# Moving one token tile from the dense group to the last Strassen group of a linear-attention and expert-mixture kernel

## The chip, the cores and the metric

The kernel runs on one core of one Trainium2 chip. The metric is the device time of one execution in microseconds, as the median of three runs.

## The reference

Linear attention over 4 batches, 8 heads, 576 positions and head size 64, followed by a dense mixture of 4 experts over the 2304 resulting tokens. Cut to what matters:

```python
def phi(x):
    proj = einsum('bhsd,df->bhsf', x, w_phi)              # 128 features
    proj = proj - max(abs(proj), axis=-1, keepdims=True)
    return concatenate([exp(proj), exp(-proj)], axis=-1)

q_p, k_p = phi(q), phi(k)
kv, z = einsum('bhsf,bhsd->bhfd', k_p, v), sum(k_p, axis=2)
x = einsum('bhsf,bhfd->bhsd', q_p, kv) / (einsum('bhsf,bhf->bhs', q_p, z)[..., None] + 1e-6)

x = x.transpose(0, 2, 1, 3).reshape(2304, 512)            # tokens x model width
p = domain_probs / (domain_probs.sum(-1, keepdims=True) + 1e-9)
for e in range(4):                                        # w1: 512 x 1024, w2: 1024 x 512
    out += p[:, e:e+1] * (maximum(x @ w1[e], 0) @ w2[e])
```

## The kernel before, in words

The 2304 tokens are 18 tiles of 128. The mixture walks over the hidden width in units: a unit is 256 hidden columns of one expert, so a pass over all experts has NU = 16 units. The tokens are split into three groups, and each group makes one pass of 16 units: units 0 to 15 for the first group, 16 to 31 for the second, 32 to 47 for the last.

- The first group (`first_units`, L586) has N0 = 4 tiles, computed densely. A unit has 2 halves of 128 hidden columns, for each half 4 slices of the model width, for each slice 3 matmuls (`terms`, L94: every factor is split into a high and a low part, and three of the four products are kept). That is 24 first-layer matmuls over 512 token columns (`l1_part`, L574). Each half ends with a relu on ScalarE (L598) and the low part of it on VectorE (`relu_lo`, L567).
- The second group (`xa`) has 8 tiles, the last (`xb`) 6. Their first layer is a Strassen-Winograd product over two halves of the tokens, 512 or 384 columns each (`strassen_unit`, L679): 7 products, named A to D by their PSUM bank, each of 2 x 3 matmuls, 42 in all. VectorE, GpSimd and ScalarE make sums of the products, the relus and the low parts (`evacuate`).
- The second layer is the same everywhere (`l2_tile`, L532): 6 matmuls of 512 columns for each tile of 128 tokens, then one VectorE operation that scales the bank by the token's probability and adds it to the output (L555). The second layer of unit n is issued during unit n + 1, from a list `pend`. In a Strassen unit one tile is issued behind each product from the second on, and what is left follows the seventh.

The first group shares TensorE with the attention. Attention is a list of steps for 16 pairs of heads (`STAGES`, L406), each with a due key; a pair has 16 keys, and pairs 0 to 3, the first batch, have to be through before the first group begins. The queue of due steps is worked off as a clock advances (`tick`, L450). The clock's step is set (L878) so that the attention from pair 4 on is spread over 88% of the ticks of the first group; a dense unit has 8 ticks for its first layer and 2 for each second-layer tile. Weight loads and their splits into parts are also placed by ticks (`load`, `convert`, W_WAIT, L67): the load of w2 for unit n + 1 goes 4 ticks behind the first layer of unit n, its split begins at the end of unit n. What each engine executes, and SyncE's DMA queue too, is in the order in which this clock issues it.

The operands of the Strassen groups (differences of token halves, T1 to T4) are made by `x_ops` (L627) on VectorE, ScalarE and GpSimd from `xd`, a copy of the attention's output in DRAM. For the second group they are issued near the end of the attention and in its first unit; for the last group in the last two units of the second. From unit 16 on `s_sums` (L474), `s_hi` and `s_lo` make the sums of weight blocks for the Strassen products, on the same three engines.

The PSUM banks: `ps_l1` 2, `ps_l2` 2, `ps_att` 3, `ps_kv` 1. Products A and B and the dense first layer use `ps_l1`; C and D use `ps_att`. Second-layer tiles use `ps_l2`; in the dense units after the attention they go by their index to `ps_l2`, `ps_att`, `ps_kv`, `ps_att`; in the Strassen units every tile whose number is a multiple of 3 goes to `ps_kv`.

The activations h of a unit lie in tiles of 128 x 2 x 512: one for each token half and for high and low part, two buffers of each.

Of the kernel before, what the change touches and what calls it, by code (L numbers as in the profile page):

```python
# [11 lines left out]
F32 = mybir.dt.float32  # L12
F32R = mybir.dt.float32r
# [7 lines left out]
def kernel(  # L21
# [25 lines left out]
    NTT = NT // P  # L47
    NPAIR = B * NP

    N0, N1 = 4, 4  # L50

# [18 lines left out]
    const = ctx.enter_context(tc.tile_pool(name="const", bufs=1))  # L70
    dram = ctx.enter_context(tc.tile_pool(name="dram", bufs=1, space=bass.MemoryType.DRAM))
    wp = ctx.enter_context(tc.tile_pool(name="wp", bufs=1))
    hp_ = ctx.enter_context(tc.tile_pool(name="hp", bufs=2))
    ps_l1 = ctx.enter_context(tc.tile_pool(name="ps_l1", bufs=2, space=PSUM))
    ps_l2 = ctx.enter_context(tc.tile_pool(name="ps_l2", bufs=2, space=PSUM))
    ps_att = ctx.enter_context(tc.tile_pool(name="ps_att", bufs=3, space=PSUM))
# [4 lines left out]
    pr = const.tile([P, NTT, NE], F32, name="pr")  # L81
    prs = const.tile([P, NTT], F32, name="prs")
    const.tile([P, 24], F32, name="gap")
    x0_hi = const.tile([P, NP, N0 * P], F32R, name="x0_hi")
    x0_lo = const.tile([P, NP, N0 * P], F32R, name="x0_lo")
    x1_hi = const.tile([P, NP, N1 * P], F32R, name="x1_hi")
    x1_lo = const.tile([P, NP, N1 * P], F32R, name="x1_lo")
    out0 = const.tile([P, N0, DM], F32, name="out0")
    xd = dram.tile([NP, P, NT], F32, name="xd")
    den_d = dram.tile([NPAIR, 2, S], F32, name="den_d")  # L90
    rec_d = dram.tile([NPAIR, 2, S], F32, name="rec_d")
# [440 lines left out]
    def l2_tile(n, h, j, tile, o):  # L532

        e = (n % NU) * 2 // NFC
        if n >= NU and tile % 3 == 0:
            ps = ps_kv.tile([P, DM], F32, name="l2", tag="kv")
        elif n < NU and clock.key > LAST_PS:

            pool, tag = ((ps_l2, "l2"), (ps_att, "att"), (ps_kv, "kv"), (ps_att, "att"))[j]
            ps = pool.tile([P, DM], F32, name="l2", tag=tag)  # L540
        else:
            ps = ps_l2.tile([P, DM], F32, name="l2", tag="l2")
        for f in range(2):
            for k, (l, r) in enumerate(terms(h, weights["w2", n])):
                nc.tensor.matmul(  # L545
                    ps, lhsT=l[:, f, j * P : (j + 1) * P], rhs=r[:, f, :],
                    start=(f == 0 and k == 0), stop=(f == 1 and k == 2),
                )
            if f == 0 and n < NU:
                tick()  # L550
        p = pr[:, tile, e : e + 1]
        if n % NU == 0:
            nc.vector.tensor_scalar_mul(o, ps, p)
        else:
            nc.vector.scalar_tensor_tensor(o, ps, p, o, op0=ALU.mult, op1=ALU.add)  # L555
        if n % NU == NU - 1:
            nc.sync.dma_start(out[tile * P : (tile + 1) * P, :], o)
# [16 lines left out]
    def l1_part(n, f, k):  # L574

        if k == 0:
            banks[n, f] = ps_l1.tile([P, 512], F32, name="l1", tag="l1")
        ksl = slice(k * P, (k + 1) * P)
        w1 = [t[:, f] for t in weights["w1", n]]
        for j, (l, r) in enumerate(terms(w1, (x0_hi, x0_lo))):  # L580
            nc.tensor.matmul(
                banks[n, f], lhsT=l[:, ksl], rhs=r[:, k, :],
                start=(k == 0 and j == 0), stop=(k == NP - 1 and j == 2),
            )

    def first_units():  # L586
        pend = []
        for n in range(NU):
            load("w1", n + 2, W_WAIT[0])
            h_hi = hp_.tile([P, 2, 512], F32R, name="h_hi", tag="h_hi")  # L590
            h_lo = hp_.tile([P, 2, 512], F32R, name="h_lo", tag="h_lo")
            for f in range(2):
                for k in range(NP):
                    l1_part(n, f, k)
                    if k < NP - 1:
                        tick()
                ps = banks.pop((n, f))
                nc.scalar.activation(h_hi[:, f], ps, AF.Relu)  # L598
                relu_lo(h_lo[:, f], ps, h_hi[:, f])
                tick()  # L600
            l1_done(n, W_WAIT[2:])
            if n:
                load("w2", n + 1, W_WAIT[1])
            for fn in pend:
                fn()
                tick()
            if pend:
                l2_done(n - 1, W_WAIT[2:])
            pend = [
                functools.partial(l2_tile, n, (h_hi, h_lo), j, j, out0[:, j]) for j in range(N0)  # L610
            ]
        return pend

# [6 lines left out]

    def x_load(x, first, nt, wait=0):
        raw = x.raw = early[0].tile([P, NP, 512], F32, name="xr", tag="xr", bufs=1)
        a = first * P
        src = xd[:, :, a : a + nt].rearrange("c p t -> p c t")
        after(wait, lambda: nc.sync.dma_start(raw[:, :, :nt], src))

# [52 lines left out]
    def strassen_unit(n, x, pend, hooks):  # L679


        nt, pool, tag = x.nt, *((hp_, "h") if n % 2 else (late[0], "h2"))
        h = [
            [pool.tile([P, 2, 512], F32R, name=f"h_{p}", tag=f"{tag}_{p}", bufs=2) for p in ("hi", "lo")]
            for _ in range(2)
        ]
        banks = {}
        c = {}
        load("w1", n + 2, 1)
# [10 lines left out]
            nc.vector.tensor_tensor(temp(name), c[a], banks[bank][:, :nt], op=ALU.add)  # L700

        def relu(f, b, src):
            nc.scalar.activation(h[b][0][:, f, :nt], src, AF.Relu)  # L703

        def lo(f, b, src, relu=True):
            hi, dst = h[b][0][:, f, :nt], h[b][1][:, f, :nt]
            if relu:
                relu_lo(dst, src, hi)
            else:
                nc.gpsimd.tensor_tensor(dst, src, hi.bitcast(F32), op=ALU.subtract)  # L710
# [60 lines left out]
    def second_units(pend):  # L771
        xs, ops = xa, None
        for n in range(NU, 3 * NU):
# [8 lines left out]
                ops = x_ops(xb)  # L782
                spread(ops["t"] + ops["t3"], 2, 1.5)
            if n == NU + 3:
                x_load(xb, xb.first, xb.nt)
                for k in range(NP):
                    after(4 + k, nc.scalar.activation, x0_hi[:, k, : xb.nt], xb.raw[:, k, : xb.nt], AF.Copy)
                    after(
                        6 + k,
                        lambda k=k: nc.vector.tensor_tensor(  # L790
                            x0_lo[:, k, : xb.nt], xb.raw[:, k, : xb.nt],
                            x0_hi[:, k, : xb.nt].bitcast(F32), op=ALU.subtract,
                        ),
                    )
            if n == NU + 6:
                x_load(xb, xb.first + xb.nt // P, xb.nt)
            h = strassen_unit(n, xs, pend, hooks)
            nj = xs.nt // P
            pend = [
                functools.partial(  # L800
                    l2_tile, n, h[b], j, xs.first + b * nj + j, (out0 if b == 0 else out1[0])[:, j]
                )
                for b in (1, 0) for j in range(nj)
            ]
        for fn in pend:
            fn()
# [3 lines left out]
    with tc.manual_schedule():  # L810
# [31 lines left out]
        run_until(FIRST)  # L842
        xa, xb = Pair(), Pair()
        xa.first, xa.nt = N0, 512
        xb.first, xb.nt = N0 + 8, 384
        for x, hi, lo in ((xa, x1_hi, x1_lo), (xb, x0_hi, x0_lo)):
            x.op = {
                "B11": (hi[:, 0:2, : x.nt], lo[:, 0:2, : x.nt]),
                "B21": (hi[:, 2:4, : x.nt], lo[:, 2:4, : x.nt]),
            }  # L850
        out1 = []

        xa_ops = {}

        def to_early():
# [4 lines left out]
                    tc.tile_pool(name="early", bufs=1, side="right", reuse_waits="tile")  # L860
                )
            )
            x_load(xa, xa.first + 4, xa.nt)
# [5 lines left out]
        def to_late():  # L869

            att_stack.close()
            late.append(ctx.enter_context(tc.tile_pool(name="late", bufs=1, reuse_waits="tile")))
            out1.append(late[0].tile([P, 4, DM], F32, name="out1"))

        later(LAST_IN, to_early)
        later(LAST + XA_LATE, to_late)
# [46 lines left out]
```

## Time and profile before

| | us |
|---|---|
| median of 3 runs | 985.53 |
| lowest and highest run | 980.63, 986.21 |
| span of the profiled execution | 981.1 |
| TensorE busy with matmuls | 962.0 (98%) |
| weight loads busy | 835.6 (85%) |
| VectorE | 658.4 (67%) |
| ScalarE | 425.8 (43%) |
| GpSimd | 524.2 (53%) |
| DMA engines, share of the main queue | 28.0% |

The profile is of one execution, with the span from its first to its last instruction; what lies around the span isn't shown. In the rows PE is TensorE with its matmuls, PEld its weight loads (they overlap the matmuls), DVE is VectorE, ACT ScalarE, POOL GpSimd, SPq the DMA queue of SyncE. Matmuls are pipelined, and the duration of one reaches over the start of the next; what a matmul costs is read from one start to the next. A row's last bracket gives the idle time of the engine before the instruction and what ended it.

### The profile page before, as it was taken

Reading aid. Unit: us, or ns where it says so; the run is one execution under the profiler, and the core shown is the slowest. Engines: PE = TensorE matmul, PEld = TensorE weight load, DVE = VectorE, ACT = ScalarE, POOL = GpSimd, SP = SyncE. Lnnn points to the kernel's source line nnn. Section 1 sums busy time; section 2 is a strip of 40 time slices with the busy share of each in tenths; the row PEclk is TensorE's granted clock in tenths of the full one; section 3 lists DMA queues with packets and bytes.
Section 4 is the critical chain, followed back from the end, with each engine's and each line's share of the span. In section 5 each row is a group of like instructions: output and inputs, shape, how many; then the busy total and the mean of one; then the engine's idle time right before and its main releaser. Section 6 shows DMA issues by size and latency. Waiting matters only on the chain. (4 is left out here: it accounts for less than half of the span.)

```text
span 981.1 us, 13542 instructions
## 1 busy us (share of the span) xinstructions
PE 962.0 (98%) x5039; PEld 835.6 (85%) x5039; DVE 658.4 (67%) x991; ACT 425.8 (43%) x768; POOL 524.2 (53%) x403
## 2 busy tenths in 40 slices
PE   8999999999999998999999999999989999999998
PEld 7888889899988887788888888888878888888887
DVE  6466656656656688867666666668876766776764
ACT  5665555555555544334333333333433434343341
POOL 3545556545454548555554555545655565665651
PEclk9899999999999999999999999999999999999999
DMA  6433434334333324221122111121132221222211
GB/s 159 124 89 80 119 96 113 93 101 123 105 105 102 110 69 132 90 93 43 48 93 65 43 43 51 58 65 43 44 118 76 65 84 47 85 65 65 65 43 65
DMA packets 70609, 80.37 MB, mean 82 GB/s; under 512 B 34160, under 2 KB 36080, under 8 KB 70544
## 3 DMA queue, kind: packets, MB, share of 16 engines
q1 hardware_dynamic: 70464, 79.48, 28.0%
q8 instruction: 40, 0.66, 0.3%
q14 instruction: 25, 0.20, 0.1%
q10 hardware_dynamic: 80, 0.03, 0.0%
HBM read 72.00 MB, written 7.49 MB: 81 GB/s over the span
## 5 line engine op out<-in xcount | busy, mean ns | idle before, releaser
L555 DVE SCALAR_TENSOR_TENSOR out<-l,pr,out 128x512 f32<-128x512 f32 x270 | 200.0, 747 | 107.4 <-PE l L545 106.4
L545 PE MATMUL l<-w2hi,h_lo 128*128 128x512 f32 x576 | 227.1, 394 | 2.7 <-DVE out L555 2.7
L545 PE MATMUL l<-w2hi,h_hi 128*128 128x512 f32 x576 | 226.5, 393 | 0.0
L545 PE MATMUL l<-w2lo,h_hi 128*128 128x512 f32 x576 | 226.2, 393 | 0.2 <-POOL w2lo L471 0.2
L508 POOL TENSOR_TENSOR w1lo<-wraw,w1hi 128x512 fp32r<-128x512 f32 x64 | 80.3, 1273 | 93.6 <-ACT w1hi L500 55.7
L545 PEld LDWEIGHTS l<-w2hi,h_hi 128*128 128x128 f32 x576 | 108.3, 188 | 23.1
L471 POOL TENSOR_TENSOR w2lo<-wraw,w2hi 128x1024 fp32r<-128x1024 f32 x48 | 115.2, 2399 | 22.5 <-ACT w2hi L465 19.0
L545 PEld LDWEIGHTS l<-w2hi,h_lo 128*128 128x128 f32 x576 | 108.5, 188 | 21.8 <-DVE out L555 4.0
L545 PEld LDWEIGHTS l<-w2lo,h_hi 128*128 128x128 f32 x576 | 108.5, 188 | 18.2 <-POOL w2lo L471 0.6
L703 ACT ACTIVATE h_hi<-c 128x512 fp32r<-128x512 f32 (+1 forms) x96 | 55.0, 578 | 68.7 <-DVE c L700 67.7
L713 POOL TENSOR_TENSOR c<-u,s 128x512 f32<-128x512 f32 (+1 forms) x32 | 37.2, 1164 | 86.6 <-DVE u L700 86.6
L257 PEld LDWEIGHTS kv<-v,e 128*128 128x128 f32 x640 | 80.0, 197 | 3.2
L257 PE MATMUL kv<-v,e 128*128 128x66 f32 x640 | 78.6, 277 | 0.0
L508 POOL TENSOR_TENSOR s_lo<-ws,s_hi 128x768 fp32r<-128x768 f32 x32 | 59.1, 1848 | 34.8 <-ACT s_hi L500 34.8
L729 ACT ACTIVATE c<-c 128x512 f32<-128x512 f32 (+1 forms) x32 | 18.5, 579 | 125.1 <-POOL c L713 125.1
L568 DVE SCALAR_TENSOR_TENSOR h_lo<-l,h_hi 128x512 fp32r<-128x512 f32 x32 | 21.9, 688 | 64.0 <-ACT h_hi L598 64.0
L207 DVE TENSOR_REDUCE m<-proj 128x4 f32<-128x512 f32 (+1 forms) x80 | 50.4, 630 | 15.9 <-PE proj L195 15.4
L710 POOL TENSOR_TENSOR h_lo<-c,h_hi 128x512 fp32r<-128x512 f32 (+1 forms) x32 | 37.5, 1173 | 40.2 <-ACT h_hi L703 40.2
L235 POOL TENSOR_TENSOR elo<-e,ehi 128x640 fp32r<-128x640 f32 x24 | 37.9, 1593 | 38.3 <-ACT ehi L227 38.2
L465 ACT ACTIVATE w2hi<-wraw 128x1024 fp32r<-128x1024 f32 x48 | 50.5, 1053 | 13.8 <-PE l L545 12.6
L209 DVE TENSOR_TENSOR d<-proj,m 128x512 f32<-128x512 f32 (+1 forms) x80 | 51.1, 638 | 4.4
L471 POOL TENSOR_TENSOR w1lo<-wraw,w1hi 128x1024 fp32r<-128x1024 f32 x16 | 38.2, 2388 | 28.8 <-ACT w1hi L465 24.4
(151 smaller groups left out, 2225.0 us busy)
## 6 DMA issues: line engine op xcount, KB each, us to landing
wraw<-in_w_dram SPq DMA_DIRECT2D x96, 512.0 KB
kq<-in_kq_dram SPq DMA_DIRECT2D x31, 256.0 KB
rb<-rec_d SPq DMA_DIRECT2D x32, 144.0 KB
out_dram<-out SPq DMA_DIRECT2D x18, 256.0 KB
v<-in_v_dram SPq DMA_DIRECT2D x32, 128.0 KB
xd<-rb SPq DMA_DIRECT2D x8, 288.0 KB
xr<-xd SPq DMA_DIRECT2D x2, 768.0 KB
kq<-in_kq_dram SPq DMA_DIRECT2D x32, 32.0 KB
```

Of the source, the lines that this page charges most:

```text
L207: nc.vector.tensor_reduce(m[:, :g], psv, axis=AX.X, op=ALU.max, apply_absolute_value=True)
L209: nc.vector.tensor_tensor(d[:, :n].rearrange("p (g f) -> p g f", f=NF), psv, m[:, :g].unsqueeze(2).to_broadcast([P, g, NF]), op=ALU.subtract,)
L235: engine.tensor_tensor(lo[sl], e[sl], parts[0][sl].bitcast(F32), op=ALU.subtract)
L257: nc.tensor.matmul(s.kv[:, n * KW : (n + 1) * KW], lhsT=e[:, e0 : e0 + NF], rhs=s.v[:, t, h * KW : (h + 1) * KW], start=(c == 0 and j == 0 ...
L465: nc.scalar.activation(hi, raw, AF.Copy)
L471: nc.gpsimd.tensor_tensor(lo, raw, hi.bitcast(F32), op=ALU.subtract)
L508: nc.gpsimd.tensor_tensor(dst, src, hi.bitcast(F32), op=ALU.subtract)
L545: nc.tensor.matmul(ps, lhsT=l[:, f, j * P : (j + 1) * P], rhs=r[:, f, :], start=(f == 0 and k == 0), stop=(f == 1 and k == 2),)
L555: nc.vector.scalar_tensor_tensor(o, ps, p, o, op0=ALU.mult, op1=ALU.add)
L703: nc.scalar.activation(h[b][0][:, f, :nt], src, AF.Relu)
L710: nc.gpsimd.tensor_tensor(dst, src, hi.bitcast(F32), op=ALU.subtract)
L713: nc.gpsimd.tensor_tensor(temp("c22"), c["u3"], c["s5"], op=ALU.add)
```

## The change

The first group gets 3 tiles in place of 4, the last 7 in place of 6; the second keeps 8, which are now tiles 3 to 10. The last group's halves have 448 columns in place of 384, so its fourth tile lies across both halves. For that the two halves of a unit's activations lie side by side in one tile of 128 x 2 x 1024, for high and low part one each; there is one such pair for odd and one for even units, and the dense units use its left and right half in turn. The second-layer matmuls take columns by their offset j. The last group's order of tiles is 4, 5, 6, 3, 0, 1, 2. The tiles x0_hi and x0_lo shrink from 512 to 448 columns.

```diff
-    N0, N1 = 4, 4
+    N0, N1 = 3, 4
+    XB = (NTT - N0 - 2 * N1) * P // 2
+    X0 = max(N0 * P, XB)
...
-    hp_ = ctx.enter_context(tc.tile_pool(name="hp", bufs=2))
+    hp_ = ctx.enter_context(tc.tile_pool(name="hp", bufs=1))
+    h_odd = [hp_.tile([P, 2, 1024], F32R, name=f"h_{k}") for k in ("hi", "lo")]
...
-            pool, tag = ((ps_l2, "l2"), (ps_att, "att"), (ps_kv, "kv"), (ps_att, "att"))[j]
+            pool, tag = ((ps_l2, "l2"), (ps_att, "att"), (ps_kv, "kv"), (ps_att, "att"))[tile]
...
-                    ps, lhsT=l[:, f, j * P : (j + 1) * P], rhs=r[:, f, :],
+                    ps, lhsT=l[:, f, j : j + P], rhs=r[:, f, :],
...
-                banks[n, f], lhsT=l[:, ksl], rhs=r[:, k, :],
+                banks[n, f][:, : N0 * P], lhsT=l[:, ksl], rhs=r[:, k, : N0 * P],
...
-            h_hi = hp_.tile([P, 2, 512], F32R, name="h_hi", tag="h_hi")
-            h_lo = hp_.tile([P, 2, 512], F32R, name="h_lo", tag="h_lo")
+            h0 = n % 2 * 512
+            h_hi, h_lo = (t[:, :, h0 : h0 + N0 * P] for t in h_odd)
...
-        nt, pool, tag = x.nt, *((hp_, "h") if n % 2 else (late[0], "h2"))
-        h = [
-            [pool.tile([P, 2, 512], F32R, name=f"h_{p}", tag=f"{tag}_{p}", bufs=2) for p in ("hi", "lo")]
-            for _ in range(2)
-        ]
+        nt = x.nt
+        h = h_odd if n % 2 else h_even
+
+        def part(k, f, b):
+            return h[k][:, f, b * nt : (b + 1) * nt]
...
-            nj = xs.nt // P
+            full, cut = 2 * xs.nt // P, xs.nt // P
+            order = [*range(-(-xs.nt // P), full), *range(cut, -(-xs.nt // P)), *range(cut)]
             pend = [
                 functools.partial(
-                    l2_tile, n, h[b], j, xs.first + b * nj + j, (out0 if b == 0 else out1[0])[:, j]
+                    l2_tile, n, h, j * P, xs.first + j, (out0 if j < 4 else out1[0])[:, j % 4]
                 )
-                for b in (1, 0) for j in range(nj)
+                for j in order
             ]
...
-        xb.first, xb.nt = N0 + 8, 384
+        xb.first, xb.nt = N0 + 2 * N1, XB
...
+            h_even.extend(late[0].tile([P, 2, 1024], F32R, name=f"h2_{k}") for k in ("hi", "lo"))
```

## Rows read from the trace of the kernel before

**Rows 1.** Busy time by stretch: us, busy us (instructions) of each engine, clock, DMA.

```profile
80.00:345.00 265.00, 265.00 (x1673) 238.03 (x1672) 164.16 (x261) 138.51 (x246) 137.63 (x112) 1.00 0.37 105
345.00:393.20 48.20, 45.34 (x212) 37.35 (x211) 41.69 (x52) 21.81 (x37) 31.65 (x19) 1.00 0.36 108
```

**Rows 2.** Timeline of PE, second group: product A of two successive units.

```profile
506.65 0.39 PE L751 MATMUL A<-x_hi,w1lo 128*128 128x512 f32 x1
...
527.05 0.39 PE L751 MATMUL A<-x_hi,w1lo 128*128 128x512 f32 x1
```

**Rows 3.** Timeline of PE, last group: a product, a second-layer tile, the next product.

```profile
742.31 0.33 PE L751 MATMUL D<-T3hi,s_lo 128*128 128x384 f32 x1
...
743.35 0.39 PE L545 MATMUL l<-w2hi,h_lo 128*128 128x512 f32 x1
...
744.74 0.33 PE L751 MATMUL C<-B22hi,s_lo 128*128 128x384 f32 x1
```

**Rows 4.** Timeline of PE, attention: six matmuls of 320 columns and their follower.

```profile
355.48 0.31 PE L332 MATMUL num<-ehi,kvlo 128*128 128x320 f32 x1
...
356.36 0.40 PE L545 MATMUL l<-w2hi,h_lo 128*128 128x512 f32 x1
```

**Rows 5.** Timelines of DVE and POOL from the first to the second group.

```profile
350.59 0.69 DVE L568 SCALAR_TENSOR_TENSOR h_lo<-l,h_hi 128x512 fp32r<-128x512 f32 x1 [1.97 <-ACT h_hi L598]
351.75 2.87 DVE L664 TENSOR_TENSOR T<-xr,x_hi 128x512 f32<-128x512 f32 x1
...
373.63 2.52 DVE L381 TENSOR_TENSOR rb<-nd,rb 64x576 f32<-64x576 f32 x2 [2.03 <-DMA rb<-rec_d]
...
382.00 1.29 DVE L568 SCALAR_TENSOR_TENSOR h_lo<-l,h_hi 128x512 fp32r<-128x512 f32 x2 [1.74 <-ACT h_hi L598]
...
388.23 4.69 DVE L555 SCALAR_TENSOR_TENSOR out<-l,pr,out 128x512 f32<-128x512 f32 x7
...
351.68 2.40 POOL L471 TENSOR_TENSOR w2lo<-wraw,w2hi 128x1024 fp32r<-128x1024 f32 x1
```

**Rows 6.** Timeline of PE in unit 16: product A, a second-layer tile, product B.

```profile
382.94 0.39 PE L751 MATMUL A<-x_hi,w1lo 128*128 128x512 f32 x1
...
390.33 0.50 PE L545 MATMUL l<-w2hi,h_lo 128*128 128x512 f32 x1 [2.65 <-DVE out L555]
...
393.19 0.39 PE L751 MATMUL B<-T2hi,s_lo 128*128 128x512 f32 x1
```

**Rows 7.** Timelines of ACT and DVE: halves of T2, and a relu.

```profile
361.67 0.63 ACT L649 ACTIVATE T2hi<-T 128x512 fp32r<-128x512 f32 x1 [4.51 <-DVE T L666]
...
365.45 0.58 ACT L598 ACTIVATE h_hi<-l 128x512 fp32r<-128x512 f32 x1
...
362.22 0.68 DVE L666 TENSOR_TENSOR T<-xr,T 128x512 f32<-128x512 f32 x1
```

**Rows 8.** Timeline of PE in unit 32: second pass of product A and what follows.

```profile
719.77 0.45 PE L751 MATMUL A<-x_hi,w1lo 128*128 128x384 f32 x1 [2.54 <-ACT s L697]
...
721.39 0.63 PE L545 MATMUL l<-w2hi,h_lo 128*128 128x512 f32 x1
...
723.88 0.34 PE L751 MATMUL D<-T3hi,s_lo 128*128 128x384 f32 x1
```

**Rows 9.** Timelines of SPq and ACT: a weight load and its first reader.

```profile
351.24 0.58 SPq L457 DMA_DIRECT2D wraw<-in_w_dram  x1
...
355.68 1.06 ACT L465 ACTIVATE w1hi<-wraw 128x1024 fp32r<-128x1024 f32 x1 [0.17 <-DMA wraw<-in_w_dram]
```

**Rows 10.** Timelines of PE and DVE, attention: transposes and the difference they read.

```profile
40.60 0.66 PE L300 MATMUL dT<-ident,d 128*128 128x128 f32 x4 [1.64 <-DVE d L209]
...
87.53 0.60 PE L300 MATMUL dT<-ident,d 128*128 128x128 f32 x4
...
337.67 0.60 PE L300 MATMUL dT<-ident,d 128*128 128x128 f32 x4
...
85.37 0.69 DVE L209 TENSOR_TENSOR d<-proj,m 128x512 f32<-128x512 f32 x1
```

More of the change, by code (lines that the diff above doesn't have):

```diff
@@ L83 @@
     const.tile([P, 24], F32, name="gap")
-    x0_hi = const.tile([P, NP, N0 * P], F32R, name="x0_hi")
-    x0_lo = const.tile([P, NP, N0 * P], F32R, name="x0_lo")
+    x0_hi = const.tile([P, NP, X0], F32R, name="x0_hi")
+    x0_lo = const.tile([P, NP, X0], F32R, name="x0_lo")
     x1_hi = const.tile([P, NP, N1 * P], F32R, name="x1_hi")
     x1_lo = const.tile([P, NP, N1 * P], F32R, name="x1_lo")
-    out0 = const.tile([P, N0, DM], F32, name="out0")
+    out0 = const.tile([P, 4, DM], F32, name="out0")
     xd = dram.tile([NP, P, NT], F32, name="xd")
@@ L596, in first_units @@
                         tick()
-                ps = banks.pop((n, f))
+                ps = banks.pop((n, f))[:, : N0 * P]
                 nc.scalar.activation(h_hi[:, f], ps, AF.Relu)
@@ L609, in first_units @@
             pend = [
-                functools.partial(l2_tile, n, (h_hi, h_lo), j, j, out0[:, j]) for j in range(N0)
+                functools.partial(l2_tile, n, h_odd, h0 + j * P, j, out0[:, j]) for j in range(N0)
             ]
@@ L622, in x_load @@
         raw = x.raw = early[0].tile([P, NP, 512], F32, name="xr", tag="xr", bufs=1)
-        a = first * P
+        a = first
         src = xd[:, :, a : a + nt].rearrange("c p t -> p c t")
@@ L702, in relu @@
         def relu(f, b, src):
-            nc.scalar.activation(h[b][0][:, f, :nt], src, AF.Relu)
+            nc.scalar.activation(part(0, f, b), src, AF.Relu)
         def lo(f, b, src, relu=True):
-            hi, dst = h[b][0][:, f, :nt], h[b][1][:, f, :nt]
+            hi, dst = part(0, f, b), part(1, f, b)
             if relu:
@@ L784, in second_units @@
             if n == NU + 3:
-                x_load(xb, xb.first, xb.nt)
+                x_load(xb, xb.first * P, xb.nt)
                 for k in range(NP):
@@ L795, in second_units @@
             if n == NU + 6:
-                x_load(xb, xb.first + xb.nt // P, xb.nt)
+                x_load(xb, xb.first * P + xb.nt, xb.nt)
             h = strassen_unit(n, xs, pend, hooks)
-            nj = xs.nt // P
+            full, cut = 2 * xs.nt // P, xs.nt // P
+            order = [*range(-(-xs.nt // P), full), *range(cut, -(-xs.nt // P)), *range(cut)]
             pend = [
                 functools.partial(
-                    l2_tile, n, h[b], j, xs.first + b * nj + j, (out0 if b == 0 else out1[0])[:, j]
+                    l2_tile, n, h, j * P, xs.first + j, (out0 if j < 4 else out1[0])[:, j % 4]
                 )
-                for b in (1, 0) for j in range(nj)
+                for j in order
             ]
@@ L851 @@
         out1 = []
+        h_even = []
         xa_ops = {}
@@ L862, in to_early @@
             )
-            x_load(xa, xa.first + 4, xa.nt)
+            x_load(xa, xa.first * P + xa.nt, xa.nt)
             xa_ops.update(x_ops(xa))
```

## The prediction

> **What bounds the kernel now.** I read the table of busy time by stretch first [rows 1]. Between 80 and 345 us, where attention and the dense group share TensorE, TensorE is busy for all 265.0 of 265 us, while VectorE is busy for 164.2 (62%), ScalarE for 138.5 and GpSimd for 137.6. The same holds inside the two Strassen groups. Only at the hand-over from the dense group to the first Strassen group, 345 to 393.2 us, is TensorE short (45.3 of 48.2) and VectorE nearly full (41.7). So inside the groups the time is the sum of matmul spacings, and at the hand-over it is VectorE's queue.
>
> Then the timeline of TensorE, start to start, since the durations overlap. One unit of the first Strassen group takes 20.40 us [rows 2]; it has 42 first-layer and 48 second-layer matmuls of 512 columns, so one takes 20.40/90 = 226.7 ns. In the last group six matmuls of 384 columns take 1.04 us, 173.3 ns each, and the six of a second-layer tile behind them 1.39 us, 231.7 ns each [rows 3]. Six of 320 columns take 0.88 us, 146.7 ns each [rows 4]. The three widths lie on a line: 64 columns cost 26.7 ns. So 448 columns cost 200.0 ns. Its neighbours bound it at 173.3 and 226.7 ns (by them the whole change would be 18 us better or worse); three points on a line leave me 1 ns either way, 0.7 us in all.
>
> **The change, part by part.** *Dense group, 16 units.* The 24 first-layer matmuls go from 512 to 384 columns: 24 x 53.4 ns = 1.28 us. One second-layer tile goes: 6 x 226.7 ns = 1.36 us. That is 2.64 us a unit, 42.2 us less.
>
> *Last group, 16 units.* 42 matmuls go from 384 to 448 columns: 42 x 26.7 ns = 1.12 us. One tile comes: 1.39 us. That is 2.51 us a unit, 40.2 us more. On TensorE alone the change is worth -42.2 + 40.2 = -2.1 us. The gain is small because Strassen spends 42 narrow matmuls where the dense form spends 24.
>
> *The hand-over.* Here the dense saving isn't all cashed. At 350.59 us VectorE has nothing left but to wait for ScalarE's relu of unit 13, so it has no backlog; from then on the operand sums of the first Strassen group keep it occupied [rows 5]. Between that point and product B of unit 16 at 393.19 us [rows 6] TensorE would lose half of unit 13's first layer (0.64), its tile (1.36), two dense units (5.28) and unit 16's leading tile (1.36): 8.6 us. VectorE loses four evictions (seven take 4.69 us, 0.67 each) and at most a quarter of 0.65 us on each of seven residuals [rows 5]: 2.7 + 1.1 = 3.8 us at most, plus the 1.74 us in which it waited for ScalarE. So of 8.6 us at least 8.6 - 5.5 = 3.1 are lost, and at most all 8.6. To place the value I follow the chain. The last pair's multiply at 373.63 us waits for a DMA that began behind VectorE's own reciprocal, so only the one eviction and the two residuals ahead of that count: 1.0 us earlier. One more eviction goes behind it, 0.7. The residual of unit 15 at 382.00 us [rows 5] then starts at about 380.3 and frees the bank of product A at 381, where TensorE would be ready at 382.94 - 7.28 = 375.7 [rows 6]: a stall of 5.3 us where there was none. Behind it come the weight sums of unit 17 and three evictions in place of four before the one buffer of ps_kv is free for unit 15's third tile; that tile starts at about 388.8 in place of 390.33, one tile follows in place of two, and product B starts at 390.2 in place of 393.19. So 3.0 of the 8.6 us arrive and 5.6 are lost. I take +5.6.
>
> How far VectorE's chain can shrink also hangs on GpSimd. One operand sum takes 2.87 us beside a 2.40 us GpSimd operation that began just before it [rows 5], where a sum of the same shape without that neighbour took 0.68 [rows 7]. The Trainium skill (SBUF — State Buffer, "Who interferes with whom") says why: a VectorE instruction with two SBUF inputs is shut out for as long as a GpSimd instruction reads SBUF. The trace agrees, 2.87 against 0.68. By that rule alone evictions taken out ahead of a blocked sum bring nothing and all 8.6 us would be lost, which makes the sum +7.0 in place of +4.0.
>
> *Entry to the last group.* Product A's second pass waits 2.54 us at 719.77 [rows 8] for a ScalarE copy queued behind weight parts, which wait for VectorE. Operand sums and their parts there become a sixth longer, some 1 us of VectorE on the way, while TensorE's three products before the wait grow by 3 x 6 x 26.7 ns = 0.5 us. So +0.5, between 0 and 2.
>
> *At nothing.* In the dense units the conversion of w2 now follows its load by 2 ticks in place of 4 (3 tiles are 6 ticks, not 8). A tick keeps its length (25.0/1.17/16 = 1.34 us now, 21.9/1.17/14 = 1.34 then, from the periods below), so 2.7 us of distance go. A weight load took 4.44 us from issue to the ScalarE instruction that waited for it [rows 9]; what hides it is that SyncE issues ahead of TensorE, and that these weights are used a whole unit later. If the cover is gone, ScalarE stands for up to 4.4 - 2.7 = 1.7 us once a unit with the relus and exponentials behind it, and TensorE meets that only if a bank of ps_l1 comes late. The new x_out slices move 128 columns of a ScalarE and a GpSimd operation from one op to the other in pairs 0 to 3 and shorten one in pairs 4 to 7; x_store of those four sends 128 KB in place of 64; the two x_load of the last group send 896 KB in place of 768, many units ahead. These lie on ScalarE and GpSimd, 52% busy at most, and on queues that run ahead [rows 1]. The order of second-layer tiles in the last group starts with columns 512 to 895, all of half 1; the tile across both halves is fourth, 5 us behind the last residual of half 0. The ps_kv bank now takes tiles 9, 3, 6 of eight and 15, 12 of seven; two uses stand at least two tiles (2.7 us) apart against a 0.75 us eviction.
>
> Sum: -2.1 + 5.6 + 0.5 = +4.0 us, from the span of 981.1 to 985.1. The profile shows nothing outside its span, and the median of the runs, 985.53, lies 4.4 above it; I put the +4.0 on the median: 989.5.
>
> **The rivals.** *The plain sum.* VectorE gives way (sums fall beside idle GpSimd, the DMA lands earlier) and the hand-over costs nothing more: -2.1, 983.4. For it: no TensorE gap from 80 to 345 us [rows 1]. Against: 41.7 us of VectorE in 48.2.
>
> *Clock.* After the wait at 719.77, six 384-column matmuls took 1.62 us in place of 1.04 and the next six of 512 took 2.49 in place of 1.39 [rows 8]: near the 1.2 GHz level, 1.7 us lost. After the wait before 390.33 the two tiles up to 393.19 took 2.86 us in place of 2.72, so the clock held [rows 6]. The two stalls of 5.3 and 3.4 us that I forecast may each bring such a fall: +3.4, 992.9. The Trainium skill (TensorE: Matmul & The Clock Gate, "HAM oscillation — how this bites in real kernels") says that a TensorE left idle between bursts begins the next one throttled; the trace agrees at 719.77 and not at 390.33.
>
> *Attention becomes late*, the other side. With less dense filler a pair's period falls: ten periods between 87.53 and 337.67 [rows 10] are 25.0 us, and 16 x 0.88/12 = 1.17 units a pair x 2.64 take off 3.1, to 21.9. A key shrinks from 1.56 to 1.37 us. The transposes stand 2.9 keys behind their projection, so they lose 0.6 us of slack; the smallest I found is 87.53 - 86.06 = 1.47 [rows 10], 0.9 is left. The place is that wait; it decides once VectorE's queue is over 0.9 us later. Ahead of the filler the same wait cost 1.64 us [rows 10]; half of that on 11 pairs is +9, 998.5.
>
> *Halves not told apart.* If second-layer matmuls of unit n had to wait for unit n+1's relu, written into the other half of the same tile, each dense unit would stand for a relu and a residual, 0.58 + 0.65 us [rows 5, 7] and hand-offs, 1.5 x 16 = +24 on the forecast, 1013. Against: ScalarE's part of T2 began at 361.67 while VectorE wrote the tile's second half only from 362.22 [rows 7], though both halves are written ahead of it in the program; waits go by region.
>
> **How the numbers follow.** Forecast 0.64 (own range 986.5 to 994.0: 3.1 and 0 to 8.6 and 2 for the two crossings), plain sum 0.15, clock 0.12, attention late 0.07, halves 0.02. The range reaches down past the plain sum to the fastest run before, 980.5, and up to half of the late attention, 997.0. About 1% (9.9 us) is what a measurement of this kernel can tell from no change. Faster by more needs the plain sum and a hand-over shorter than now: 0.03. Slower by more: late attention, halves and the top of the forecast, 0.12. Within: 0.85.
>
> **What would show it.** Matmul spacing of 173 ns in the dense units and 200 ns in the last group; units of 18.1 us there in place of 15.6; a dense stage without TensorE gaps up to unit 14; then waits of 4 to 6 us at product A of unit 16 (for ScalarE or VectorE) and 3 us at the third tile behind it. TensorE waits for L209 or L235 during attention would prove the late chain; product B close behind unit 15's tiles would prove the plain sum. A 448-column matmul off the line by 5 ns would break the sum by 3.4 us.

## The result and the profile after

The changed kernel takes 988.83 us (median of 20 runs, 983.21 to 995.03), and the kernel before, run beside it, 982.19 (20 runs, 978.46 to 987.30): a ratio of 1.0064, 95% interval 1.0046 to 1.0081. So it is 0.6% slower. The interval leaves out "no change", the size stays under the 1% that the prediction gave as what a measurement can tell, and the sign is the one that was forecast. In microseconds it is 6.3 to 6.6 more, where +4.0 was forecast. That 989.5 lies so near to 988.83 is in part luck: the 985.53 on which the +4.0 was put is 3.3 us above what the kernel before showed beside the changed one.

Both profiles are compared from the first dense matmul, since the kernel before ran its first 80 us some 2.5 us longer, at a granted clock of 0.66 between 40 and 50 us. Timeline of PE of the changed kernel: first dense matmul, first matmul of the last dense unit (unit 15), product A of unit 16, of unit 18, and of two successive units of the last group; they answer to [rows 2, 3, 6]. The lines of the code lie three or four further down than before.

```profile
77.23 0.33 PE L584 MATMUL l<-x_hi,w1lo 128*128 128x384 f32 x1
...
331.77 0.33 PE L584 MATMUL l<-x_hi,w1lo 128*128 128x384 f32 x1
...
344.51 0.47 PE L755 MATMUL A<-x_hi,w1lo 128*128 128x512 f32 x1 [0.61 <-POOL s_lo L511]
...
386.68 0.39 PE L755 MATMUL A<-x_hi,w1lo 128*128 128x512 f32 x1
...
933.61 0.36 PE L755 MATMUL A<-x_hi,w1lo 128*128 128x448 f32 x1
...
951.75 0.36 PE L755 MATMUL A<-x_hi,w1lo 128*128 128x448 f32 x1
```

And of the kernel before, the first dense matmul, the first of the last dense unit, and product A of unit 18:

```profile
79.75 0.39 PE L581 MATMUL l<-x_hi,w1lo 128*128 128x512 f32 x1
...
372.06 0.39 PE L581 MATMUL l<-x_hi,w1lo 128*128 128x512 f32 x1
...
425.05 0.39 PE L751 MATMUL A<-x_hi,w1lo 128*128 128x512 f32 x1
```

From the first dense matmul to unit 18 the change saves 345.30 - 309.45 = 35.85 us. From there to the end of the span it costs (983.4 - 386.68) - (981.1 - 425.05) = 40.67 us. Together +4.8 us, where the sum said +4.0. The rest of the measured 6.3 to 6.6 goes with the clock: the 20 runs of the changed kernel had a mean granted clock of 0.9918, and the 71 runs of the kernel before that stood beside all experiments 0.9943. Within the runs of one kernel the time goes with that clock, about 0.9 us for each 0.001 in the kernel before (0.987 to 0.998, 989 to 976 us) and 0.7 in the changed one. Put to the same clock of 0.995, before is 981.3 us, and after is 985.8 by the first slope and 986.5 by the second: +4.5 to +5.2. Whether the change lowers the clock itself, by its waits, isn't settled.

Where the saving goes shows at the start of the last dense unit. It begins 292.31 us after the first dense matmul before and 254.54 after: up to there 37.8 us are saved, about all that the smaller units can give by then (37.4, from 2.58 us a unit as measured below). From there to unit 18 the kernel before takes 52.99 us; with the smaller units 49.1 would be left, and the changed kernel takes 54.91. So 5.8 us are lost at the hand-over: 4.4 as far as product A of unit 16 (12.74 us, where a dense unit takes 8.30) and 1.4 behind it.

The table of busy time by stretch, columns as in [rows 1]: attention beside the dense group, and the hand-over as far as product B of unit 16.

```profile
80.00:310.00 230.00, 228.66 (x1584) 218.11 (x1583) 155.95 (x248) 134.22 (x244) 135.45 (x109) 1.00 0.41 121
310.00:355.00 45.00, 38.26 (x188) 32.69 (x187) 37.57 (x45) 20.95 (x37) 31.90 (x19) 0.96 0.38 120
```

Up to 310 us TensorE lacks 1.3 us of 230, in two waits for ScalarE, 0.69 us at 83.87 and 0.65 at 248.73, where before it lacked nothing. In the hand-over it lacks 6.7 of 45.0, where before it lacked 2.9 of 48.2 [rows 1], and the mean clock is 0.96 where it was 1.00.

Where it stands: timeline of PE in units 15 and 16, the longer waits (in the bracket, how long and for whom) and what follows the longest.

```profile
334.63 0.44 PE L584 MATMUL l<-x_hi,w1lo 128*128 128x384 f32 x1 [0.58 <-DVE h_lo L571]
...
342.24 0.50 PE L548 MATMUL l<-w2hi,h_lo 128*128 128x512 f32 x1 [2.50 <-DVE out L558]
...
344.51 0.47 PE L755 MATMUL A<-x_hi,w1lo 128*128 128x512 f32 x1 [0.61 <-POOL s_lo L511]
...
352.22 0.80 PE L548 MATMUL l<-w2hi,h_lo 128*128 128x512 f32 x1 [2.65 <-DVE out L558]
352.81 0.63 PE L548 MATMUL l<-w2lo,h_hi 128*128 128x512 f32 x1
...
354.52 0.63 PE L548 MATMUL l<-w2hi,h_hi 128*128 128x512 f32 x1
354.95 0.53 PE L755 MATMUL B<-T2hi,s_lo 128*128 128x512 f32 x1
...
363.33 0.47 PE L755 MATMUL D<-T4hi,w1lo 128*128 128x512 f32 x1 [1.25 <-DVE u L704]
```

The wait of 2.65 us before 352.22 was there before too [rows 6]; new are the 0.58, the 2.50 at the third tile of unit 14 (the one dense tile of three in ps_kv) and the 0.61. After the wait of 2.65 us the matmuls from 352.81 to 354.52 start 0.43 us apart in place of 0.23, at a granted clock of 0.50: the lower level, 1.2 GHz. That tile takes 2.73 us where six matmuls at full clock take 1.36; with 0.1 us for the start behind a wait, the fall costs some 1.2 us, most of what is lost behind product A.

And the queues behind it: timelines of SPq, DVE and POOL in the same stretch, for the last attention pair (other instructions of the three stand between).

```profile
320.65 0.57 SPq L355 DMA_DIRECT2D den_d<-nd  x2
322.61 0.35 SPq L360 DMA_DIRECT2D den<-den_d  x1
329.51 0.20 DVE L365 RECIPROCAL rec<-den 128x9 f32<-128x9 f32 x1
329.74 0.33 SPq L368 DMA_DIRECT2D rec_d<-rec  x1
330.05 4.06 DVE L670 TENSOR_TENSOR xr<-xr 128x512 f32<-128x512 f32 x2
330.70 2.85 POOL L474 TENSOR_TENSOR w2lo<-wraw,w2hi 128x1024 fp32r<-128x1024 f32 x1
331.16 1.71 SPq L374 DMA_DIRECT2D rb<-rec_d  x2
332.96 0.54 SPq L460 DMA_DIRECT2D wraw<-in_w_dram  x1
334.49 3.12 DVE L384 TENSOR_TENSOR rb<-nd,rb 64x576 f32<-64x576 f32 x2
338.98 0.47 DVE L484 TENSOR_TENSOR ws<-wraw 128x256 f32<-128x256 f32 x1
```

This is a chain: the denominators go out to memory and come back, are inverted, go out and come back again as the reciprocals; only then comes the multiply (L384) and, behind it in VectorE's order, the weight sums of unit 16 (L484), whose parts product A needs. The raw weights of unit 16 are issued on the same in-order SyncE queue behind the reciprocals (332.96). From the write of the denominators to product A of unit 16 it takes 23.9 us here and took 25.9 before (357.02 to 382.94), though each of the two dense units that lie whole in between got 2.58 us shorter: of 5.2 us, 2.1 arrived.

### The profile page after: what moved, and what is told of

Same layout as the page of the kernel before. It is cut to its first block, busy times and chain, and to the rows that moved or that the text cites. A ratio compares the mean times of both kernels' runs of the same rounds, so it can differ in the third digit from the quotient of the medians.

```text
span 983.4 us, 13577 instructions
## 1 busy us (share of the span) xinstructions
PE 956.6 (97%) x5039; PEld 837.4 (85%) x5039; DVE 669.9 (68%) x991; ACT 428.5 (44%) x768; POOL 524.5 (53%) x403
## 5 line engine op out<-in xcount | busy, mean ns | idle before, releaser
L511 POOL TENSOR_TENSOR w1lo<-wraw,w1hi 128x512 fp32r<-128x512 f32 x64 | 76.9, 1221 | 74.7 <-issue 68.0
L717 POOL TENSOR_TENSOR c<-u,s 128x512 f32<-128x512 f32 (+1 forms) x32 | 39.5, 1235 | 107.4 <-DVE u L704 107.4
L707 ACT ACTIVATE h_hi<-c 128x512 fp32r<-128x512 f32 (+1 forms) x96 | 57.6, 605 | 67.5 <-DVE c L704 64.7
L260 PEld LDWEIGHTS kv<-v,e 128*128 128x128 f32 x640 | 77.3, 192 | 1.5
L260 PE MATMUL kv<-v,e 128*128 128x66 f32 x640 | 76.2, 271 | 0.0
L571 DVE SCALAR_TENSOR_TENSOR h_lo<-c,h_hi 128x512 fp32r<-128x512 f32 (+1 forms) x64 | 72.0, 1125 | 2.5 <-ACT h_hi L707 2.5
L714 POOL TENSOR_TENSOR h_lo<-c,h_hi 128x512 fp32r<-128x512 f32 (+1 forms) x32 | 39.7, 1241 | 43.8 <-ACT h_hi L707 43.8
L704 DVE TENSOR_TENSOR u<-s,B 128x512 f32<-128x512 f32 (+1 forms) x32 | 20.9, 654 | 61.4 <-issue 35.5
L468 ACT ACTIVATE w2hi<-wraw 128x1024 fp32r<-128x1024 f32 x48 | 50.2, 1046 | 11.5 <-PE l L548 6.2
```

Of the source, the lines that this page charges most:

```text
L260: nc.tensor.matmul(s.kv[:, n * KW : (n + 1) * KW], lhsT=e[:, e0 : e0 + NF], rhs=s.v[:, t, h * KW : (h + 1) * KW], start=(c == 0 and j == 0 ...
L468: nc.scalar.activation(hi, raw, AF.Copy)
L571: nc.vector.scalar_tensor_tensor(lo, src, 0.0, hi.bitcast(F32), op0=ALU.max, op1=ALU.subtract)
L707: nc.scalar.activation(part(0, f, b), src, AF.Relu)
```

## The experiments

Beside each: "A" is the start of product A of unit 16 after the first dense matmul, "U" that of unit 18, from the same rows as above. Before: A 303.19, U 345.30. After: A 267.28, U 309.45. The kernel before stood at 980.9 to 981.9 us beside the experiments.

| kernel | median us | A | U |
|---|---|---|---|
| layout_only | 982.8 | 303.03 | 345.94 |
| dense_only | 944.4 | 266.58 | 308.85 |
| last_only | 1020.9 | 303.23 | 345.39 |
| att_bank | 987.9 | 266.89 | 309.34 |
| spread_84 | 988.7 | 268.66 | 310.14 |
| spread_78 | 989.4 | 273.57 | 312.90 |
| wraw3 | 987.2 | 267.14 | 309.01 |
| fewer_sums | 986.1 | 265.23 | 307.16 |
| t3_late | 990.2 | 267.01 | 310.57 |
| no_chain | 983.2 | 263.52 | 305.89 |
| t_after | 991.3 | 269.24 | 310.93 |
| late_pair | 992.9 | 265.39 | 307.85 |

A and U are from one profiled execution each; those of t3_late and spread_78 were the slowest of their kernel (993.6 and 994.5 us). Also, the kernels with three dense tiles that pace attention alike reach the last dense unit between 253.6 and 254.5 us, and nearly all of that difference arises in the first dense unit, far ahead of the hand-over. So A is safer counted from the start of the last dense unit. It is 12.7 to 12.8 us in the changed kernel, att_bank, wraw3 and t3_late, 11.5 in fewer_sums, 11.1 in late_pair and 9.6 in no_chain; a dense unit without loss is 8.3.

**The parts: layout_only, dense_only, last_only.**

```
layout_only:  N0, N1 = 3, 4   ->  N0, N1 = 4, 4
dense_only:   XB = (NTT - N0 - 2 * N1) * P // 2   ->  XB = 384
last_only:    N0, N1 = 4, 4;  XB = 448;  xb.first = 11
```

> The side-by-side activation tiles, the new second-layer indexing and the new order of tiles, but with four dense tiles and six last ones as before. Region theory (waits go by the part of a tile that is written): same time as before within 2 us, dense units of 10.88 us and last units of 15.66 us. Rival (halves of one tile are not told apart): TensorE waits of 1.2 us or more in each dense unit, some 20 us more.

> Three dense tiles, but still six last ones (tiles 11 to 16); tile 17 is left out, so its rows of the output are not written. Hand-over theory (VectorE's queue between the dense and the first Strassen group eats what TensorE saves behind the attention): 42.2 us saved in the units, 6 to 8 us given back at the hand-over, 34 to 36 us less than before. Plain sum: 42 us less. Clock theory (the excess over the forecast comes from half-clock stretches anywhere): 42 less 2 to 3, and the profile's hand-over no longer than before.

> The dense group keeps four tiles and the last group takes seven, so tile 11 is computed twice and stands in the output as the last group made it. If the two sizes act each by itself, this is the cost of the last group alone: 16 units by 2.47 to 2.51 us = 39.5 to 40.2, and 1 to 3 us for the waits at the entry to the last group: 1022 to 1026 us beside 981.9, a ratio of 1.041 to 1.045; with the dense part alone (-37.5) that adds up to the +6.5 measured. If the two parts press on each other (the seven-tile group dear only because the dense stage got short), it is 1018 or less and the sum of the parts is short of +6.5 by 3 us or more.

Measured: layout_only 1.0014 (0.9988 to 1.0040) of before, with units of 20.40 and 15.66 us as before and no wait in a dense unit behind attention: the two halves in one tile cost nothing that can be told. dense_only 0.9610 (0.9580 to 0.9641), -37.5 us, more than the 34 to 36 of the hand-over theory and less than the plain sum. last_only 1.0391 (1.0369 to 1.0414), +39.3 us, a little under what was expected (1022 to 1026, measured 1020.9). The medians add up to +1.8 and not to +6.5. But last_only's four runs had a clock of 0.9972, far above the 0.9918 of the changed kernel. At 0.995, by 0.9 us for each 0.001, the parts are -37.4 and +41.7, together +4.3, and the whole is +4.5: by that working the two sizes act each by itself, and what is left goes with the clock. Whether last_only's high clock belongs to it or to four lucky runs isn't settled.

**Which wait it is: att_bank, spread_84, wraw3.**

```
att_bank:   ((ps_l2, "l2"), (ps_att, "att"), (ps_kv, "kv"), (ps_att, "att"))[tile]
            -> ((ps_l2, "l2"), (ps_att, "att"), (ps_att, "att"))[tile]
spread_84:  SPREAD = 0.88 -> 0.84
wraw3:      tag="wraw", bufs=2 -> bufs=3
```

> The changed kernel with the third dense second-layer tile behind the attention in a ps_att bank (three buffers) in place of ps_kv (one). Queue theory (VectorE and GpSimd have too much to do there, and the bank is only where TensorE meets it): the waits of 2.5 and 2.65 us at the third tile go, but come back at product A and at products 6 and 7 of unit 16; 0 to 1.5 us faster than the changed kernel. Bank theory (one buffer of ps_kv is the cause): 4 to 5 us faster.

> The changed kernel with the attention spread over 84% of the dense ticks in place of 88%: 8 ticks of 0.59 us, 4.8 us, more dense work behind the attention. Hand-over theory: TensorE has that much more to do while VectorE catches up, 3 to 5 us faster than the changed kernel, 1.001 to 1.003 of the kernel before. Late-chain theory (attention is at its limit): TensorE waits appear from 77 to 300 us and eat the gain, same as the changed kernel or slower.

> The changed kernel with three buffers for raw weights in place of two, nothing else. If the loads that wait for a raw buffer (four issues of 338.07 took 12.54 us on SyncE) set the hand-over, the sums of the weights of units 16 and 17 start earlier, the stalls of 2.50 us at 342.24 and 2.65 us at 352.22 shrink by 2 us or more together, and the time is 985 to 987. If VectorE and GpSimd set it by their own work, the stalls stay within 1 us of these and the time is 988 to 989.

None helped: 1.0048 (1.0024 to 1.0072), 1.0069 (1.0043 to 1.0094), 1.0058 (1.0037 to 1.0079). In att_bank the wait of 2.50 us at the third tile is gone, and there are these in its place (timeline of PE):

```profile
343.74 0.76 PE L755 MATMUL A<-x_hi,w1lo 128*128 128x512 f32 x1 [3.40 <-DVE h_lo L571]
362.39 0.47 PE L755 MATMUL D<-T4hi,w1lo 128*128 128x512 f32 x1 [3.21 <-DVE u L704]
```

So the bank only shows the wait, as the queue theory had it; U stays at 309.3. A third raw buffer leaves U within 0.5 us: the number of the loads' buffers doesn't set it either. And spread_84, which leaves more dense work behind attention, missed its 3 to 5 us: it moves the wait to another tile (3.23 us at 336.84 in its trace).

**VectorE's sums or the round trip: fewer_sums, t3_late.**

```
fewer_sums:  xa_ops["t"][2:4] = [];  for k in ("t", "T2", "T1", "t3", "T3") -> ("t", "T2", "T1", "T3")
t3_late:     for k in ("t", "T2", "T1", "t3", "T3") -> ("t", "T2", "T1")      # at LAST_IN
             for k in ("B22", "t4", "T4") -> ("t3", "T3", "B22", "t4", "T4")  # at XA_START
```

> The changed kernel with four of the sums of the first Strassen group left out on VectorE (the second pass over T1 and both sums of T3, so that the operands T1 and T3 of the first Strassen group are not the right ones): in the trace of the changed kernel they took 1.29 and 4.06 us there, just ahead of the product with the reciprocals. If VectorE's queue sets the hand-over, A of unit 16 starts 2.5 to 4 us earlier against the dense start than the 267.3 us of the changed kernel, and the time is 985 to 986.5. If the weight loads (two raw buffers, SyncE's order) set it, A of unit 16 stays within 1 us and the time is 988 to 989.

> The changed kernel with the sums and the split of T3 of the first Strassen group taken out from ahead of the last pair's product with the reciprocals and put behind the hand-over, ahead of B22 and T4. If it is GpSimd's T3 halves beside VectorE and VectorE's own T3 sums that hold up the chain, A of unit 16 comes 1.5 to 3.5 us earlier (by the 1.6 us that the product took more beside GpSimd and some of the 4.06 us of the sums) and the time is 985.5 to 987.5, as long as T3 and T4 are ready when unit 16 asks for them. If they are late there, the gain is given back at product D of unit 16: 988 to 990.

fewer_sums came to 986.1 us (1.0040, 1.0017 to 1.0063), A 2.05 us earlier where 5.35 us of sums were gone; t3_late to 990.2 (1.0070, 1.0050 to 1.0090), A where it was. Timeline of DVE in t3_late: the sums of T3 are out of the way, and the multiply stands all the same.

```profile
335.43 0.20 DVE L365 RECIPROCAL rec<-den 128x9 f32<-128x9 f32 x1
...
339.91 0.75 DVE L384 TENSOR_TENSOR rb<-nd,rb 64x576 f32<-64x576 f32 x1 [3.40 <-DMA rb<-rec_d]
341.33 0.76 DVE L384 TENSOR_TENSOR rb<-nd,rb 64x576 f32<-64x576 f32 x1 [0.67 <-DMA rb<-rec_d]
...
343.44 0.41 DVE L484 TENSOR_TENSOR ws<-wraw 128x256 f32<-128x256 f32 x1
```

It now waits for the reciprocals to come back, 4.5 us after the reciprocal. In the changed kernel the 4.06 us of T3's sums had filled that same time, so taking them out brings the multiply forward by only 0.5 us against the start of the last dense unit. What fewer_sums gained, it gained by what it took out ahead of the reciprocal, which ran 249.85 us after the dense start in place of 252.28 (0.8 us of that, and of the 2.05, was there before the last dense unit began); there the multiply waited 3.98 us for the same transfer. So of my two theories neither held as written. VectorE's work ahead of the reciprocal counts; what stands between the reciprocal and the multiply is nearly hidden by the way out to memory and back.

The same round trip holds up a second thing. Timeline of ACT in t3_late, the first reader of unit 16's raw weights:

```profile
343.04 0.94 ACT L503 ACTIVATE w1hi<-wraw 128x512 fp32r<-128x512 f32 x2 [8.18 <-DMA wraw<-in_w_dram]
```

Their load was issued at 338.88, behind the reciprocals in SyncE's order, and they were there 4.2 us later; the first weight sum, at 343.44, could hardly have come earlier, whatever the multiply did.

**The round trip itself: no_chain, spread_78, t_after.**

```
no_chain (on t3_late):  if i == NPAIR - 1 and fn in (den_out, den_in, den_recip, rec_out): continue
                        if i == NPAIR - 1 and fn is rec_in: o = 20;  rec_d[i] -> rec_d[i - i // (NPAIR - 1)]
spread_78:  SPREAD = 0.88 -> 0.78
t_after:    X_IN = 4 -> 8
```

> The kernel t3_late with the last pair's round trip of the denominators left out: for that pair the denominators are not written, read, inverted or written back, and the reciprocals are loaded early, from the pair before it (so the last pair's share of the output is not the right one). In t3_late the last pair's product waited 3.40 and 0.67 us for these loads. If this chain of transfers is what the shorter dense stage no longer covers, the product comes 4 to 8 us earlier, A of unit 16 starts 262 to 264 us after the dense start (267.0 in t3_late, 267.3 in the changed kernel) and the time is 982 to 986. If the work of VectorE and GpSimd itself sets the hand-over, A of unit 16 stays at 266 to 267 and the time is 988 to 990.

> The changed kernel with SPREAD 0.78 in place of 0.88: attention is paced to end earlier against the dense units, so more dense work is left to run while the last pair's reciprocals go out and come back. If the round trip sets the hand-over, A of unit 16 starts up to 4 us earlier (263 to 265 us after the dense start) and the time is 984 to 987. If an attention paced that fast falls behind on VectorE, ScalarE and GpSimd, waits of 1 us and more turn up between attention's matmuls and the time is 990 to 998. If it is neither, 988 to 989 as with 0.84.

> The changed kernel with the operands of the first Strassen group begun four steps of the plan later (X_IN 8 in place of 4), so that the halves of T2 and the sums of T3 stand behind the last pair's reciprocal and its product on VectorE. If the reciprocal's place behind the sums is what makes the round trip late (it ran at 329.51 us, 6.9 us after the read of the denominators was issued at 322.61), the reciprocal comes 2 to 4 us earlier, A of unit 16 starts 264 to 265.5 us after the dense start and the time is 985.5 to 987.5. If T2, T3 or T4 are late instead, the wait moves to unit 16's products and the time is 988 to 991.

no_chain: 983.2 us, 1.0024 (0.9998 to 1.0050) of before; A 3.5 and U 4.7 us earlier than in t3_late, 3.8 and 3.6 earlier than in the changed kernel. Timelines of SPq, DVE and PE in no_chain (its lines lie four further down):

```profile
320.99 4.48 SPq L464 DMA_DIRECT2D wraw<-in_w_dram  x2
...
331.14 3.78 DVE L384 TENSOR_TENSOR rb<-nd,rb 64x576 f32<-64x576 f32 x2
...
339.44 0.50 PE L552 MATMUL l<-w2hi,h_lo 128*128 128x512 f32 x1 [0.22 <-DVE out L562]
341.76 0.47 PE L759 MATMUL A<-x_hi,w1lo 128*128 128x512 f32 x1 [0.66 <-DVE h_lo L575]
...
349.43 0.52 PE L552 MATMUL l<-w2hi,h_lo 128*128 128x512 f32 x1 [2.66 <-DVE out L562]
```

The multiply waits for nothing, though it is slower (3.78 us beside GpSimd), and ahead of product B the one long wait left is the 2.66 us that the kernel before has too. Counted from the last dense unit, A comes 3.1 us earlier than in the changed kernel, and U 2.9. Against t3_late A comes as much earlier, but there a fall of the clock stands ahead of A; unit 14's third tile, ahead of that fall, comes 2.7 us earlier. So the round trip of one pair is worth about 3 of the 5.8 us lost at the hand-over; the other half stays open, save the fall of the clock, some 1.2 us in the changed kernel, which no_chain has too (behind its 2.66 us). The runs of no_chain also had a higher clock (0.9948 against 0.9918), which goes with some 2 to 3 us of the 5.6 by which its median is lower. And no_chain doesn't tell the two ways of the round trip apart: it takes away the multiply's wait and also lets the weight load go early (320.99). No run moved the load alone.

Neither way to shorten it within the plan came out. In spread_78 the multiply ran 248.8 us after the dense start, 8.5 earlier, and product A still not: TensorE went into it without a wait, having lost its time ahead of it, in waits of 1.34 us at 248.44 and 2.82 at 334.27, in shorter ones during attention, and at a granted clock of 0.67 from 330 to 340 us. The 1.34 is the sign of an attention that falls behind. 989.4 us, 1.0084 (1.0054 to 1.0115). In t_after the reciprocal came 251.83 us after the dense start, 0.45 earlier and not 2 to 4: with the halves of T2 moved back, T1's sums stood in front of it instead. The wait at unit 14's third tile grew to 5.04 us; 991.3, 1.0103 (1.0068 to 1.0138). My expectation of that run was wrong.

**A version with nothing left out: late_pair.**

```
if i == NPAIR - 1:
    o += {den_in: 22, den_recip: 28, rec_out: 28, rec_in: 30, x_mul: 37, x_store: 37}.get(fn, 0)
nd, den, rec of the last pair: from wp;  rb: in the buffer of xr
if n >= NU and tile % 3 == 0:  ->  tile % 3 == 1:
```

> The changed kernel with two edits and nothing left out. The last pair's read of its denominators, its reciprocal, the two loads of it, the product and the store are put 22 to 37 steps of the plan later, behind the weight sums of units 16 and 17 (only the last token group needs this pair, 300 us later), in tiles of their own. And of the tiles of the Strassen groups the ones with number 1 modulo 3 go to the bank ps_kv, in place of 0 modulo 3, so that the last tile of the one group and the first of the next don't both want it. If the round trip of the last pair is what the shorter dense stage no longer covers, A of unit 16 starts 262 to 264.5 us after the dense start (267.3 in the changed kernel), as with the round trip left out, unit 33 falls from 18.97 to 18.1 to 18.4, and the time is 981 to 984, the same as before the change or up to 1 us under it. If VectorE's other work in front of the weight sums sets the hand-over, A stays at 266 to 267 and the time is 987 to 989; if the round trip put behind the sums now holds up unit 16 or 17, A is early and the time still 986 to 990.

It took 992.9 us, 1.0132 (1.0089 to 1.0175), and the expectation missed, in a place that neither theory had. A came 1.9 and U 1.6 us earlier, less than without the round trip, since the weight sums, at last begun at 334.27, ran beside GpSimd until 338.4. Unit 33 fell from 18.97 to 18.34, which is what its neighbours take. But every unit of the Strassen groups got longer: 20.85 us in place of 20.40, 18.36 in place of 18.13. Timeline of PE in late_pair, six matmuls of 512 columns in the first Strassen group:

```profile
404.70 0.40 PE L764 MATMUL A<-x_hi,w1lo 128*128 128x512 f32 x1
...
406.09 0.40 PE L764 MATMUL B<-T2hi,s_lo 128*128 128x512 f32 x1
```

1.39 us for six, 231.7 ns each, at a granted clock of 1.00, where it was 226.7 [rows 2]. Fifteen units of each group make 15 x 0.45 + 15 x 0.23 = 10.2 us. Without that it would stand at about 982.7, still 1.8 us above the 980.9 of the kernel before beside it; that is worked out and not measured. What of the edit makes the matmuls slower is open: it also moves where the tiles behind it lie in SBUF, and that wasn't tried by itself.

## Why the prediction was right, and where it was not

*Dense units.* A dense unit behind attention takes 8.30 us in the changed kernel and was 48 x 226.7 ns = 10.88. That is 2.58 and not 2.64. Timeline of PE, the last dense unit but one: 17 matmuls of 384 columns, then 18 of 512.

```profile
324.70 0.33 PE L584 MATMUL l<-x_lo,w1hi 128*128 128x384 f32 x1
...
327.65 0.39 PE L548 MATMUL l<-w2hi,h_lo 128*128 128x512 f32 x1
...
331.77 0.33 PE L584 MATMUL l<-x_hi,w1lo 128*128 128x384 f32 x1
```

2.95 / 17 = 173.5 ns, as the line through the widths said; but 4.12 / 18 = 228.9 ns for the second layer, 2 ns more than taken. Over 16 units the saving is 41.3 us and not 42.2.

*Last group.* A unit takes 18.14 us (933.61 to 951.75), 2.47 more than the 15.66 of the kernel before, where 2.51 was forecast; the 448-column matmuls lie 202 ns apart on the mean of that group, 2 off the line, and the second layer's 229 in place of 231.7 [rows 3] made up for it. 39.5 us against 40.2.

*The hand-over.* From the last dense unit to unit 18, 5.8 us were lost, where +5.6 was forecast; of the 41.3 us 35.85 arrived, since the stage ahead saved 0.4 more than its units, attention's two waits included. So the size was right, and nearer than its working deserves: 1.2 of the 5.8 is a fall of the clock, which the forecast didn't hold. The working was right in part. The bounds, 3.1 to 8.6, held, and so did the statement that the last pair's multiply waits for a DMA behind VectorE's own reciprocal and hardly moves. But I took it for VectorE's backlog and put 5.3 us of waiting on product A of unit 16, behind the residuals of unit 15. There it was 0.61; the wait came a unit earlier, 2.50 us at unit 14's third tile, whose bank is emptied behind the multiply. What failed is the step that names the cause: the runs show that taking VectorE's sums away gives 1.2 us, a bank nothing, a raw buffer nothing, and taking the round trip of the denominators away about 3 of the 5.8. The rest is not shown. In these runs the way from the reciprocal to the multiply took 4.5 to 5.3 us whether VectorE had work meanwhile or not (t3_late, fewer_sums, t_after, and 5.0 in the changed kernel). When the matmuls that hide such a transfer get shorter, it doesn't get shorter with them, and saving is lost there.

*GpSimd beside VectorE.* Two operand sums took 4.06 us at 330.05 beside GpSimd, where one alone takes 0.68 [rows 7]: by the Trainium skill (SBUF — State Buffer, "Who interferes with whom") VectorE is shut out there, and the trace agrees. But the +7.0 that the rule by itself would have given was too much: the blocked 4 us were in the main time in which the multiply had to wait for its transfer anyway (t3_late).

*Entry to the last group.* +0.5 was forecast, and 40.67 - 39.5 = 1.2 came, in another place. Timeline of PE:

```profile
666.81 0.50 PE L548 MATMUL l<-w2hi,h_lo 128*128 128x512 f32 x1 [1.17 <-DVE out L558]
683.84 0.47 PE L755 MATMUL A<-x_hi,w1lo 128*128 128x448 f32 x1 [2.59 <-ACT s L701]
700.18 0.50 PE L548 MATMUL l<-w2hi,h_lo 128*128 128x512 f32 x1 [0.55 <-DVE out L558]
```

The 2.54 us [rows 8] stayed, 2.59, without the fall of the clock behind it, which the kernel before had there; unit 32 is 1.2 us shorter than its wider matmuls would make it. Unit 31 grew by 1.5 us (20.68 to 22.18) with the 1.17 at 666.81. New is the 0.55 at 700.18, which with what follows makes unit 33 0.83 us longer than its neighbours. I had put this at nothing, since two uses of ps_kv stood at least two tiles apart; I counted within each group and not across them. Tile 6 is the last of the one group and tile 15 the first of the next, both on ps_kv. In last_only the last tile of the one group is 7 and goes to ps_l2, and its unit 33 takes the 18.14 us of its neighbours; late_pair, with another remainder, has no such wait either.

*The clock.* As a rival it had 0.12 and a price of 3.4 us, beside the forecast and not in it. It came in small: one fall, behind the wait of 2.65 us at 352.22, some 1.2 us, and in the 20 runs a mean clock 0.0025 lower than before, about 2 us. The rule of the Trainium skill named there (TensorE: Matmul & The Clock Gate, "HAM oscillation — how this bites in real kernels") held in this profile at 352.22 and not at 342.24 and 683.84, after waits of 2.50 and 2.59 us: a wait of that length may bring a fall, and doesn't each time.

*At nothing.* The weights' later conversion, x_out, the stores and the two halves in one tile cost nothing that shows: layout_only's 1.0014 says so for the last of them, and for the others the 37.8 us that had arrived by the last dense unit. Attention became late by the two waits, 1.3 us, a seventh of what that rival had, and the same stage made up for them; by what, isn't shown.

## What to carry to other kernels

When a change shortens the work of one engine, look for what that work was hiding, and measure it by leaving it out: here a round trip through memory of one pair, worth about 3 of the 5.8 us lost, while banks and buffers gave nothing. Look also at what stands behind such a transfer in the same queue: here the weights of the next stage. A wait names the engine that signalled last; taking that engine's work away (t3_late) showed a transfer behind it. And where two stages share a rotating buffer, count its uses across the border too.

## What was unexpected in the hardware

Matmuls of one shape didn't have one spacing here: 512 columns took 226.7 ns in the first Strassen group, 228.9 in the dense units, and 231.7 in late_pair, whose only differences there are where tiles lie and which bank a third of the second layer's outputs use; which of them it is, no run shows. At 2% of the matmul stream, 10 us here, it outweighed all that the change was about.
